# Where the sums of w2 run, in which order x and w1 are loaded, and when late statistics may start, in an FNet and MLP kernel

## The chip, the cores and the metric

The kernel runs on one core of one Trainium2 chip. The metric is the device time of one execution, in microseconds (us).

## The reference

The input x has 2048 rows (tokens) of 576 features. It is normalized, and the output is x plus two branches of the normalized xn:

```
xn = (x - mean) / sqrt(var + 1e-5)              # over the 576 features
a  = xn @ dft_hid_re.T ;  b = xn @ dft_hid_im.T  # Fourier branch
A  = dft_seq_re @ a - dft_seq_im @ b             # 2048 x 2048 matrices
B  = max(xn @ w1, 0) @ w2                        # w1 576 x 4608, w2 4608 x 576
out = x + A + B
```

All inputs are float32, and w1 and w2 have eight times the usual spread.

## The kernel before, in words

TensorE (PE) multiplies in float16. To keep the accuracy, an operand is scaled by a power of two and split into a high and a low float16 part: ScalarE writes the high part (L164), VectorE (DVE) the low part (L165), and PE forms three of the four products. The larger products also use Winograd's form of Strassen's scheme: of two 2 x 2 block matrices, 7 products instead of 8, with sums and differences of blocks as operands.

The MLP branch comes first. The 4608 hidden features are 9 blocks `b` of 512; the 2048 rows are 4 groups `g` of 512, each of 4 tiles `t` of 128 rows. A step (b, g) is `mlp1` (4 column tiles of w1, N=512, L286), `mlp1_out`, which turns a pair of its results into operands for Strassen, once for each of the two pairs (ReLU, high parts, low parts, sums, and last the difference L314 that gives the low part of the sums), and `mlp2`, 7 products (L328), each followed by an addition on VectorE into the accumulator `acc` (L334). The loop over steps issues `mlp1` of step n together with `mlp2` of step n-1.

What block 0 needs in addition is what the change is about:

- `load_x(t)` loads a tile of x into `acc`; `load_w1(b, i)` and `load_w2(b, i)` load halves of a block of w1 and w2 into one of two `raw` buffers, so that w2 waits until w1 has been split.
- `stats(ts)` takes mean and variance of tiles (L182 bn_stats, L185 aggregation), a square root on ScalarE (L192), and a chain of small VectorE steps (L193 to L204). `normalize` (L224 on VectorE, L225 on ScalarE), `remainder` (L229 and L232, on GpSimd, called POOL in the profile, except for tile 0) and `transposes` (9 on PE, L240, and two ScalarE copies out of PSUM, L245 and L248) then fill `xT[g]`. A group's `mlp1` needs the whole `xT[g]`; only for the first group and half of the second is it done tile by tile (`tile_by`).
- `max_w1` takes the largest magnitude of w1 (L98 on VectorE), `power_w1` makes the scale from it through PE (`power_pe`, L140 to L155), `split_w1` splits.
- `prepare_w2` sums magnitudes of w2 on ScalarE (L374), makes scales (`power_w2`), splits the first parts of w2 (`split_w2` with c=0), then forms the sums of w2's blocks in place (`sums_w2`, L404 to L407), and splits these (c=1 and 2). `mlp2` needs all of it.

Transposes, `mlp2` and `power_pe` share two PSUM buffers (`ps2`).

The text of the kernel is not the order on an engine. A scheduler at compile time orders each engine's instructions: the earlier in the text, the more urgent, but an instruction that its model takes to be ready goes ahead of one that isn't. `tc.issue_after(ins)` puts what a block issues on the engine of `ins` behind `ins` in that engine's order. On the chip each of VectorE, ScalarE and POOL works through its list in order.

Of the kernel before, what the change touches and what calls it, by code (L numbers as in the profile page):

```python
# [1 line left out]

# [7 lines left out]
F32 = mybir.dt.float32  # L10
BF16 = mybir.dt.bfloat16
I32 = mybir.dt.int32
AF = mybir.ActivationFunctionType
ALU = mybir.AluOpType
# [3 lines left out]
P = 128  # L18
# [10 lines left out]
TG = G // P  # L29
GH = G // 2  # L30
KT = 5
# [10 lines left out]
def kernel(  # L42
# [17 lines left out]
    nc = tc.nc  # L60

    const = ctx.enter_context(tc.tile_pool(name="const", bufs=1))
# [14 lines left out]
    raws = {}  # L77

    def load_x(t):
        nc.sync.dma_start(acc[t], x[t * P : (t + 1) * P, :])  # L80
# [2 lines left out]
        r = raws[key] = raw.tile(shape, F32, tag="raw", name="raw_" + "_".join(map(str, key)))  # L83
        nc.sync.dma_start(r, src)

    def load_w1(b, i, parts=1, eng=nc.sync):
        r = raws["w1", b, i] = raw.tile([P, 2 * KT, P], F32, tag="raw", name=f"raw_w1_{b}_{i}")
        n = 2 * KT // parts
        for k in range(0, 2 * KT, n):
            eng.dma_start(r[:, k : k + n], w1[b, i][:, k : k + n])  # L90

    def load_w2(b, i):
        load_raw(("w2", b, i), w2[b, i], [P, 4, EH])
# [2 lines left out]
    def magnitude(dst, src):  # L96

        nc.vector.tensor_reduce(dst, src, AX.XY, ALU.max, apply_absolute_value=True)  # L98
# [18 lines left out]
    idle = const.tile([P, 256], F16, name="idle")  # L117
# [41 lines left out]
    def cell(tag, n=NQ):  # L159
        return small.tile([P, n], F32, tag=f"c_{tag}", name=f"c_{tag}", bufs=2)  # L160
# [9 lines left out]
    means, factors, shifts, order = {}, {}, {}, {}  # L170

    eps = const.tile([P, 1], F32, name="eps")
    nc.vector.memset(eps, EPS)

    def stats(ts):

        n = len(ts)
        mv = small.tile([P, n, 2], F32, tag=f"mv{n}", name=f"mv{ts[0]}")
        sts = [small.tile([P, 2, 6], F32, tag="st", name=f"st{t}", bufs=4) for t in ts]
        for t, st in zip(ts, sts):  # L180
            for j in range(2):
                nc.vector.bn_stats(st[:, j, :], acc[t][:, j * EH : (j + 1) * EH])  # L182
                yield
        for i, st in enumerate(sts):
            nc.vector.bn_aggr(mv[:, i], st.rearrange("p a b -> p (a b)"))  # L185
            yield
        r0, u, r, sh = (
            small.tile([P, n], F32, tag=f"{a}{n}", name=f"{a}_{ts[0]}") for a in ("r0", "u", "r", "sh")
        )
        m, v = mv[:, :, 0], mv[:, :, 1]  # L190
        stt = nc.vector.scalar_tensor_tensor
        nc.scalar.activation(u, v, AF.Sqrt, bias=eps)  # L192
        nc.vector.reciprocal(r0, u)  # L193
        yield

        stt(u, v, EPS, r0, ALU.add, ALU.mult)
        yield
        nc.vector.tensor_tensor(u, u, r0, ALU.mult)
        yield
        nc.vector.tensor_scalar(u, u, -0.5 * SX, 1.5 * SX, ALU.mult, ALU.add)  # L200
        yield
        nc.vector.tensor_tensor(r, u, r0, ALU.mult)
        yield
        stt(sh, m, -1.0, r, ALU.mult, ALU.mult)  # L204
        for i, t in enumerate(ts):
            means[t], factors[t], shifts[t] = mv[:, i, 0:1], r[:, i : i + 1], sh[:, i : i + 1]

    def weave(steps, *others):

        others = list(others)  # L210
        for _ in steps:
            if others:
                others.pop(0)()
        for f in others:
            f()
# [80 lines left out]
    def mlp1_out(b, g, i, pa, pb):  # L296

        h = hs[b, g, i] = mlp.tile([P, 2, 7, GH], F16, tag="h", name=f"h{b}_{g}_{i}", bufs=4)
        st = mlp.tile([P, 5, GH], F32, tag="stage", name=f"s{b}_{g}_{i}")
        stt = nc.vector.scalar_tensor_tensor  # L300
        a11, a21, a12, a22 = pa[:, :GH], pa[:, GH:], pb[:, :GH], pb[:, GH:]
        r21, s1, s2, s3, s4 = (st[:, n] for n in range(5))
        nc.scalar.activation(r21, a21, AF.Relu)  # L303
        for q, src in ((slice(A11, A11 + 1), a11), (slice(A12, A22 + 1), pb)):
            hi, lo = (h[:, n, q].rearrange("p a b -> p (a b)") for n in range(2))
            nc.scalar.activation(hi, src, AF.Relu)  # L306
            stt(lo, src, 0.0, hi, ALU.max, ALU.subtract)  # L307
        stt(s3, a11, 0.0, r21, ALU.max, ALU.subtract)
        stt(s1, a22, 0.0, r21, ALU.max, ALU.add)
        stt(s2, a22, 0.0, s3, ALU.max, ALU.subtract)  # L310
        stt(s4, a12, 0.0, s2, ALU.max, ALU.subtract)  # L311
        hi, lo = (h[:, n, S1 : S4 + 1] for n in range(2))
        order["s"] = nc.scalar.activation(hi, st[:, 1:], AF.Copy).ins  # L313
        nc.vector.tensor_tensor(lo, st[:, 1:], hi, ALU.subtract)  # L314

    places = {}

# [21 lines left out]
    sc, pw, mx = {}, {}, {}  # L339

    def max_w1(b, f):

        i, r = divmod(f, 2)
        if f == 0:
            mx["w1", b], sc["w1", b], pw["w1", b] = cell("mw1"), cell("sw1"), cell("pw1")
        if r == 0:
            mx["f", b] = cell("mf", 2)
            mx["b", i] = small.tile([P, 1], BF16, tag=f"mb{i}", name=f"mb{b}_{i}") if b < 2 else None
        magnitude(mx["f", b][:, r : r + 1], raws["w1", b, i][:, r * KT : (r + 1) * KT])
        if r:  # L350
            m = mx["w1", b][:, i : i + 1] if b > 1 else mx["b", i]
            nc.vector.tensor_reduce(m, mx["f", b], AX.X, ALU.max)

    def power_w1(b, i):
        s, p = (t["w1", b][:, i : i + 1] for t in (sc, pw))
        if b > 1:
            power(s, p, mx["w1", b][:, i : i + 1])
        else:
            power_pe(s, p, mx["b", i])
# [40 lines left out]
    def sums_w2(b, i):  # L400

        b12, b11, b21, b22 = (raws["w2", b, i][:, n] for n in range(4))
        tt = (nc.vector if b > 1 else nc.gpsimd).tensor_tensor
        tt(b11, b12, b11, ALU.subtract)  # L404
        tt(b12, b22, b12, ALU.subtract)
        tt(b22, b22, b11, ALU.subtract)
        tt(b21, b21, b22, ALU.subtract)  # L407
# [35 lines left out]
        )  # L443


    load_w1(0, 0, 2, nc.scalar)
    warm = const.tile([P, 1], F32, name="warm")
    nc.scalar.activation(warm, eps, AF.Sqrt)
    load_x(0)
    load_x(1)  # L450
    load_w1(0, 1)
    for t in range(2, 2 * TG):
        load_x(t)
    load_w2(0, 0)
    load_w2(0, 1)
    for t in range(2 * TG, NT):
        load_x(t)

    V, GP = nc.vector, nc.gpsimd
    ps = [ps1.tile([P, G], F32, tag="ps1", name=f"p1_0_0_{i}") for i in range(NF)]  # L460
# [6 lines left out]
    no = lambda: None  # L467
    N, E, T = normalize, remainder, transposes

    for _ in range(32):  # L470
        nc.tensor.matmul(ps[3][:, :256], idle[:, :P], idle, start=True, stop=True)

    weave(stats([0]), no, no, no, lambda: max_w1(0, 0))
    N(0)
    max_w1(0, 1)
    E(0, V)
    power_w1(0, 0)
    T(0)
    split_w1(0, 0)
    tile_by(0, (0,), ps, WK0)  # L480
# [53 lines left out]
    def work():  # L534
        if todo:
            todo.pop(0)()
# [5 lines left out]
    def load_d(j):  # L542
        load_raw(("d", j), dft[:, :, j * EH : (j + 1) * EH], [P, KT, EH])
# [12 lines left out]
    def split_d(j):  # L556
        split(dsp[j][:, 0], dsp[j][:, 1], raws["d", j], sc["d"][:, j : j + 1])
# [47 lines left out]
    for n in range(1, len(steps)):  # L605
        b, g = steps[n]
        pb, pg = steps[n - 1]
        if g == 0 and b:
            if b + 1 < NB:
                todo += prepare_block(b + 1)  # L610
            else:
                todo += [lambda: (load_d(0), load_d(1)), lambda: None, new_d, lambda: None]
                for j in range(4):
                    todo += [lambda j=j: power_d(j), lambda j=j: split_d(j)]
                    if j < 2:
                        todo += [lambda j=j: load_d(j + 2), lambda: None]
                todo += [scales_d]
        if b == 0 and g + 1 < NG:
            weave(stats([(g + 1) * TG + i for i in range(TG)]))
        ps = []  # L620
        for i in range(NF):
            if n > 1 or i > 1:
                ps.append(mlp1(b, g, i))
                if i % 2:
                    mlp1_out(b, g, i // 2, *ps[-2:])
            if b == 0 and g + 1 < NG:
                t = (g + 1) * TG + i
                normalize(t)
                remainder(t, nc.gpsimd)
                transposes(t)  # L630
            if n == 2 and i == 2:
                todo += prepare_block(1)
            for _ in range(1 if b else 3):
                work()
            for q in range(2 * i, min(2 * i + 2, 7)):
                mlp2(pb, pg, q)
            for _ in range(1 if b else 3):
                work()
            if n > 3 and i % 2 and passes:
                passes.pop(0)()  # L640
# [115 lines left out]
    for n, (p, kh) in enumerate(units):  # L756
# [4 lines left out]
        for i, (q, rq, first, row, col) in enumerate(PRODUCTS):  # L761
# [5 lines left out]
            ps, w = places[PLACE[i]], csp[m]  # L767
            for k in range(HK):
                r = R[kh * HK + k]
                for j, (a, c) in enumerate(((0, 0), (0, 1), (1, 0))):  # L770
                    nc.tensor.matmul(  # L771
                        ps, w[:, a, k], r[:, c, rq],
                        start=first and k == 0 and j == 0, stop=k == HK - 1 and j == 2,
# [63 lines left out]
```

## Time and profile before

| | |
|---|---|
| median of 3 runs | 1306.94 us (1304.04 to 1307.52) |
| profiled execution: time | 1306.57 us |
| profiled execution: span | 1304.8 us |
| mean granted clock of PE | 0.991 |
| PE busy | 1274.5 us, 98% of the span |
| VectorE busy | 968.0 us, 74% |
| ScalarE busy | 532.8 us, 41% |
| POOL busy | 49.7 us, 4% |

The span is the time between the first and the last instruction of the profiled execution; the rest of its time, 1.77 us, lies around it. In rows of the trace, a row with times gives start and duration, engine, line, operation, what it writes and reads, and in brackets how long the engine had stood and what ended that. "Granted clock" is the share of full speed that PE was given.

### The profile page before, as it was taken

The numbers are of one execution on the slowest core, as the hardware profiler recorded it, in microseconds if no ns is written. First come the engines' busy times: TensorE is split into PE (matmuls) and PEld (weight loads), VectorE is DVE, ScalarE is ACT, GpSimd is POOL, SyncE is SP. The second block draws the span as 40 slices with busy tenths as digits, with TensorE's granted clock in tenths as the row PEclk, the third lists the DMA queues.
The fourth block names the chain that finished last, engine by engine and source line by source line (L and its number), as shares of the span: only waits on it lengthen the run. The fifth ranks groups of instructions, "written<-read, shape, count | busy, mean of one in ns | idle before, by whom it ended". The sixth has DMA issues, their size and how long they took to land.

```text
span 1304.8 us, 21675 instructions
## 1 busy us (share of the span) xinstructions
PE 1274.5 (98%) x9066; PEld 871.2 (67%) x9066; DVE 968.0 (74%) x1655; ACT 532.8 (41%) x794; POOL 49.7 (4%) x76
## 2 busy tenths in 40 slices
PE   7799999999999999999999999999999999999998
PEld 6565566666666666666666656677777777777777
DVE  8857778577596686785875885568678887878875
ACT  5634344344343443533433433234443333333332
POOL 2412000000000000000000000000000000000000
PEclk8899899999999999999999999999999999999999
DMA  6101213122122131131221222240014334243420
GB/s 238 42 1 55 76 49 116 58 73 87 48 89 85 49 107 68 49 125 49 74 93 41 94 94 85 91 149 17 1 52 172 131 128 159 98 146 121 142 84 19
DMA packets 38002, 112.75 MB, mean 86 GB/s; under 512 B 3984, under 2 KB 10640, under 8 KB 37904
## 3 DMA queue, kind: packets, MB, share of 16 engines
q1 hardware_dynamic: 37616, 110.71, 25.4%
q8 instruction: 71, 1.16, 0.4%
q10 hardware_dynamic: 288, 0.66, 0.1%
q14 instruction: 27, 0.22, 0.1%
HBM read 101.91 MB, written 9.44 MB: 85 GB/s over the span
## 4 chain that ended last, share of the span: by engine, by line
PE 89%; DVE 5%; ACT 2%; POOL 2%; DMA 1%; issue 1%; POOLq 0%; ACTq 0%; SPq 0%; DVEq 0%
PE p L286 30%; PE p L328 25%; PE p L771 25%; PE pd L670 8%; DVE acc L334 1%; DMA raw_d<-in_dft_dram 1%; ACT xT L245 0%; DVE h L314 0%; DVE w2s L165 0%; DVE h L307 0%; DMA raw_w<-in_w_dram 0%; POOL raw_w L407 0%; PE pt L240 0%; DVE c_md L98 0%; POOL raw_w L404 0%
## 5 line engine op out<-in xcount | busy, mean ns | idle before, releaser
L286 PE MATMUL p<-xT,w1s 128*128 128x512 f16 (+1 forms) x2268 | 466.3, 359 | 4.6 <-ACT xT L245 4.5
L328 PE MATMUL p<-w2s,h 128*128 128x288 f16 x3024 | 397.7, 288 | 14.3 <-ACT xT L248 7.8
L328 PEld LDWEIGHTS <-h 128*128 128x128 f16 x3024 | 296.8, 98 | 117.1 <-issue 15.3
L286 PEld LDWEIGHTS <-w1s 128*128 128x128 f16 x2268 | 210.0, 99 | 209.1 <-issue 9.1
L771 PE MATMUL p<-R,cs 128*128 128x288 f16 x2688 | 329.4, 287 | 0.0
L771 PEld LDWEIGHTS <-cs 128*128 128x128 f16 x2688 | 262.9, 98 | 66.3
L334 DVE SCALAR_TENSOR_TENSOR acc<-p,c_ub,acc 128x576 f32<-128x576 f32 x252 | 204.0, 812 | 19.3 <-PE p L328 18.9
L164 ACT ACTIVATE cs<-c,sc_c 128x1024 f16<-128x1024 f32 x112 | 128.5, 1148 | 202.0 <-PE p L771 147.6
L307 DVE SCALAR_TENSOR_TENSOR h<-p,h 128x256 f16<-128x256 f32 (+1 forms) x144 | 80.0, 555 | 148.6 <-ACT h L306 148.3
L165 DVE SCALAR_TENSOR_TENSOR cs<-c,sc_c,cs 128x1024 f16<-128x1024 f32 x112 | 143.7, 1283 | 50.2 <-ACT cs L164 42.9
L306 ACT ACTIVATE h<-p 128x256 f16<-128x256 f32 (+1 forms) x144 | 69.5, 485 | 236.9 <-PE p L286 236.9
L313 ACT ACTIVATE h<-s 128x1024 f16<-128x1024 f32 x72 | 76.1, 1058 | 166.6 <-DVE s L311 166.3
L670 PE MATMUL pd<-dsp,xT 128*128 128x288 f16 x896 | 109.9, 287 | 0.9 <-DVE acc L334 0.9
L314 DVE TENSOR_TENSOR h<-s,h 128x1024 f16<-128x1024 f32 x72 | 88.9, 1235 | 28.7 <-ACT h L313 28.6
L670 PEld LDWEIGHTS <-xT 128*128 128x128 f16 x896 | 87.6, 98 | 23.2 <-issue 1.1
L777 DVE SCALAR_TENSOR_TENSOR o<-p,us_c,o 128x288 f32<-128x288 f32 x112 | 57.5, 513 | 20.3 <-PE p L771 20.3
L598 ACT ACTIVATE f<-f 128x1024 f32<-128x1024 f32 x64 | 66.6, 1041 | 3.6 <-DMA f<-in_cre_dram 3.6
L165 DVE SCALAR_TENSOR_TENSOR w2s<-raw_w,c_sw,w2s 128x576 f16<-128x576 f32 (+1 forms) x54 | 48.2, 940 | 16.0 <-ACT w2s L164 16.0
L164 ACT ACTIVATE w2s<-raw_w,c_sw 128x576 f16<-128x576 f32 (+1 forms) x54 | 44.4, 850 | 36.7 <-DVE c_sw L396 19.0
L303 ACT ACTIVATE s<-p 128x256 f32<-128x256 f32 x72 | 26.7, 370 | 24.0 <-PE p L286 24.0
L688 ACT ACTIVATE R<-pd,c_rho 128x288 f16<-128x288 f32 x48 | 23.8, 499 | 22.2 <-DVE T L682 12.4
L165 DVE SCALAR_TENSOR_TENSOR w1s<-raw_w,c_sw,w1s 128x640 f16<-128x640 f32 x36 | 30.9, 878 | 0.1
(100 smaller groups left out, 623.8 us busy)
## 6 DMA issues: line engine op xcount, KB each, us to landing
f<-in_cre_dram SPq DMA_DIRECT2D x32, 512.0 KB, 3.5
f<-in_cim_dram SPq DMA_DIRECT2D x32, 512.0 KB, 3.5
c<-in_cre_dram SPq DMA_DIRECT2D x32, 512.0 KB, 3.9
c<-in_cim_dram SPq DMA_DIRECT2D x32, 512.0 KB, 4.5
raw_w<-in_w_dram SPq DMA_DIRECT2D x17, 640.0 KB, 4.0
raw_w<-in_w_dram SPq DMA_DIRECT2D x18, 576.0 KB, 4.0
acc<-in_x_dram SPq DMA_DIRECT2D x16, 288.0 KB, 6.1
spill<-acc SPq DMA_DIRECT2D x16, 288.0 KB, 2.5
```

Source lines behind the costliest of these rows:

```text
L164: nc.scalar.activation(hi, src, AF.Copy, scale=s)
L165: nc.vector.scalar_tensor_tensor(lo, src, s, hi, ALU.mult, ALU.subtract)
L286: nc.tensor.matmul(ps[:, cols], w1s[b, i // 2][:, hl, i % 2 * KT + k], xT[g][:, kx, cols], start=(n == 0), stop=(n == len(WK) - 1),)
L306: nc.scalar.activation(hi, src, AF.Relu)
L307: stt(lo, src, 0.0, hi, ALU.max, ALU.subtract)
L313: order["s"] = nc.scalar.activation(hi, st[:, 1:], AF.Copy).ins
L314: nc.vector.tensor_tensor(lo, st[:, 1:], hi, ALU.subtract)
L328: nc.tensor.matmul(ps[:, c], h[:, x, qa, c * P : (c + 1) * P], w[:, y, qb], start=first and i == 0 and j == 0, stop=i == NQ - 1 and j == 2 ...
L334: nc.vector.scalar_tensor_tensor(o, ps, us[b], o, ALU.mult, ALU.add)
L598: nc.scalar.activation(f, f, AF.Abs, scale=2.0**-10, accum_out=sums_c[:, n, q : q + 1])
L670: nc.tensor.matmul(ps[j], xT[g][:, kx, c * P : (c + 1) * P], dsp[j][:, hl, k], start=(n == 0), stop=(n == len(XK) - 1),)
L771: nc.tensor.matmul(ps, w[:, a, k], r[:, c, rq], start=first and k == 0 and j == 0, stop=k == HK - 1 and j == 2, skip_group_check=not first,)
```

## The change

Four things are done:

- `sums_w2` runs on VectorE for all blocks; before, blocks 0 and 1 ran it on POOL.
- The first half of w1 is loaded from SP's queue, like x, and no longer from ScalarE's: tile 0 of x, w1 in two parts, tiles 1 and 2 of x, the second half of w1, the other tiles.
- The statistics of the third and fourth group are put behind `order["lo"]`, the last difference (L314) of the pair that was issued last in the text, in VectorE's order. For the third group this is the first pair of step (0, 1), for the fourth the second pair of it. The maxima of w1 of block 1 are put behind it too: its first half behind the first pair of step (0, 2), its second half behind the second pair.
- 14 more matmuls on an idle tile stand between the first scale of w1 and the transposes of tile 0.

```diff
-    def load_w1(b, i, parts=1, eng=nc.sync):
+    def load_w1(b, i, parts=1):
...
-            eng.dma_start(r[:, k : k + n], w1[b, i][:, k : k + n])
+            nc.sync.dma_start(r[:, k : k + n], w1[b, i][:, k : k + n])
...
-        nc.vector.tensor_tensor(lo, st[:, 1:], hi, ALU.subtract)
+        order["lo"] = nc.vector.tensor_tensor(lo, st[:, 1:], hi, ALU.subtract).ins
...
-        magnitude(mx["f", b][:, r : r + 1], raws["w1", b, i][:, r * KT : (r + 1) * KT])
+        with tc.issue_after(order["lo"]) if b == 1 else nullcontext():
+            magnitude(mx["f", b][:, r : r + 1], raws["w1", b, i][:, r * KT : (r + 1) * KT])
...
-        tt = (nc.vector if b > 1 else nc.gpsimd).tensor_tensor
+        tt = nc.vector.tensor_tensor
...
-    load_w1(0, 0, 2, nc.scalar)
-    warm = const.tile([P, 1], F32, name="warm")
-    nc.scalar.activation(warm, eps, AF.Sqrt)
     load_x(0)
+    load_w1(0, 0, 2)
     load_x(1)
+    load_x(2)
     load_w1(0, 1)
-    for t in range(2, 2 * TG):
+    for t in range(3, 2 * TG):
         load_x(t)
...
+    warm = const.tile([P, 1], F32, name="warm")
+    nc.scalar.activation(warm, eps, AF.Sqrt)
...
-    for _ in range(32):
-        nc.tensor.matmul(ps[3][:, :256], idle[:, :P], idle, start=True, stop=True)
+    def fill(n):
+
+        for _ in range(n):
+            nc.tensor.matmul(ps[3][:, :256], idle[:, :P], idle, start=True, stop=True)
+
+    fill(32)
...
     power_w1(0, 0)
+    fill(14)
     T(0)
...
         if b == 0 and g + 1 < NG:
-            weave(stats([(g + 1) * TG + i for i in range(TG)]))
+            with tc.issue_after(order["lo"]):
+                weave(stats([(g + 1) * TG + i for i in range(TG)]))
```

More of the change, by code (lines that the diff above doesn't have):

```diff
@@ L1 @@
-from contextlib import ExitStack
+from contextlib import ExitStack, nullcontext
 import concourse.bass as bass
```

## The prediction

> **What bounds the kernel now.** I read the page's busy times first, then a table of stretches, then the waits of PE, then the order of time at the two places where PE waited longest.
>
> ```profile
> span 1304.8 us, 21675 instructions
> PE 1274.5 (98%) x9066; PEld 871.2 (67%) x9066; DVE 968.0 (74%) x1655; ACT 532.8 (41%) x794; POOL 49.7 (4%) x76
> ```
>
> PE is the bound of the whole: 1304.8 - 1274.5 leaves 30.3 us in which it did nothing. The other engines matter only where they make PE idle, or cold. The stretches say where that is (columns: busy time and count of PE, PEld, DVE, ACT, POOL; granted clock; DMA share; GB/s):
>
> ```profile
> 0.00:20.00 20.00, 13.67 (x110) 10.76 (x110) 16.44 (x70) 9.36 (x15) 1.61 (x6) 0.83 0.86 311
> 20.00:40.00 20.00, 17.43 (x293) 16.38 (x292) 19.00 (x67) 16.68 (x30) 9.29 (x12) 1.00 0.23 79
> 40.00:60.00 20.00, 12.36 (x100) 7.74 (x98) 14.53 (x27) 13.34 (x22) 14.30 (x16) 0.85 0.17 52
> 60.00:80.00 20.00, 17.05 (x128) 11.52 (x127) 15.09 (x32) 9.02 (x15) 4.79 (x8) 0.89 0.04 15
> 80.00:100.00 20.00, 20.00 (x145) 12.61 (x143) 10.20 (x20) 6.63 (x12) 0.86 (x1) 1.00 0.00 1
> 120.00:140.00 20.00, 16.06 (x79) 8.51 (x78) 15.36 (x27) 5.38 (x9) 9.05 (x9) 0.83 0.20 66
> 200.00:400.00 200.00, 200.00 (x1254) 122.52 (x1253) 147.90 (x280) 80.75 (x139) 2.84 (x8) 1.00 0.25 82
> ```
>
> From 200 us on PE is full and at clock 1.00. Nearly all that can be won lies in the first 140 us: 19.49 us idle in the first 80, 3.94 in 120 to 140, and more where the clock is 0.83 to 0.89. The change touches nothing that PE waits for later (from the third block on the sums of w2 are on VectorE already). From 20 to 40 us DVE is 95% busy and is the likely limit; from 40 to 60 and from 120 to 140 PE and DVE are both idle in part while POOL works, the mark of a chain through POOL.
>
> The waits of PE in the first 140 us (total, times, longest), and the order of time at the two longest:
>
> ```profile
> PE p L328 <- ACT xT L248: 7.8, 2, 6.9
> PE p L328 <- DVE acc L334: 3.9, 2, 3.4
> ```
>
> ```profile
> 46.92 1.60 POOL L404 TENSOR_TENSOR raw_w<-raw_w 128x288 f32<-128x288 f32 x1 [2.19 <-DVE w2s L165]
> ...
> 54.67 1.19 POOL L407 TENSOR_TENSOR raw_w<-raw_w 128x288 f32<-128x288 f32 x1
> 55.89 0.78 ACT L164 ACTIVATE w2s<-raw_w,c_sw 128x576 f16<-128x576 f32 x1 [1.75 <-POOL raw_w L407]
> 56.58 0.26 ACT L248 ACTIVATE xT<-pt 128x128 f16<-128x128 f16 x1
> 56.88 5.00 PE L328 MATMUL p<-w2s,h 128*128 128x288 f16 x24 [6.86 <-ACT xT L248]
> ...
> 128.29 1.37 POOL L407 TENSOR_TENSOR raw_w<-raw_w 128x288 f32<-128x288 f32 x1
> 129.70 0.77 ACT L164 ACTIVATE w2s<-raw_w,c_sw 128x576 f16<-128x576 f32 x1 [1.94 <-POOL raw_w L407]
> 130.50 0.82 DVE L165 SCALAR_TENSOR_TENSOR w2s<-raw_w,c_sw,w2s 128x576 f16<-128x576 f32 x1 [1.49 <-ACT w2s L164]
> 132.50 0.81 DVE L334 SCALAR_TENSOR_TENSOR acc<-p,c_ub,acc 128x576 f32<-128x576 f32 x1
> 133.37 3.04 PE L328 MATMUL p<-w2s,h 128*128 128x288 f16 x12 [3.40 <-DVE acc L334]
> ```
>
> Block 0: the sums on POOL run from 46.92 to 55.86. ScalarE's splits wait for them one by one, and behind the last in ScalarE's order stands L248, a 0.26 us copy that frees the PSUM buffer PE waits for. PE stood 6.86 us. Block 1: the same through DVE. Its w2 split waits for ScalarE, that for POOL, and the addition at 132.50 which frees PE's next buffer is queued behind: 3.40 us. After such a stop PE is slow:
>
> ```profile
> 57.00:60.50 3.50, 3.50 (x16) 2.18 (x15) 1.91 (x2) 2.26 (x5) 1.42 (x2) 0.50 0.60 196
> 133.40:139.20 5.80, 5.80 (x20) 2.73 (x20) 5.80 (x12) 1.60 (x3) 0.38 (x1) 0.50 0.15 64
> ```
>
> At half clock, 3.5 us cost 1.75 us and 5.8 us cost 2.9 us on top of the stops.
>
> **The change, part by part.** The sum is made against the profiled execution's own 1306.57 us, which lies 0.37 us below the median of the runs shown (1306.94). The rows of its terms follow; the stretches show PE alone (length, busy, count, clock, DMA share, GB/s):
>
> ```profile
> 13.20:43.70 30.50, 26.16 (x408) 0.95 0.34 116
> 43.70:74.26 30.56, 20.75 (x148) 0.89 0.14 44
> 118.00:140.00 22.00, 18.06 (x94) 0.84 0.18 60
> ```
>
> ```profile
> L404 DVE TENSOR_TENSOR raw_w<-raw_w x14: 447/450/460, 190.8 to 728.2; 128x288 f32<-128x288 f32 x14
> L182 DVE BATCH_NORM_STATS2 st<-acc 128x6 f32<-128x288 f32 x19 | 7.4, 442 | 0.0
> L224 DVE TENSOR_SCALAR xn<-acc,mv,r 128x576 f32<-128x576 f32 x6 | 3.2, 576 | 0.0
> L185 DVE BATCH_NORM_AGGREGATE mv<-st 128x2 f32<-128x12 f32 x12 | 1.4, 172 | 0.0
> L98 DVE TENSOR_REDUCE c_mf<-raw_w 128x1 f32<-128x640 f32 x4 | 3.2, 805 | 0.0
> L232 POOL TENSOR_TENSOR xn<-xn 128x512 f16<-128x512 f32 x15 | 18.0, 1198 | 0.0
> L229 POOL TENSOR_TENSOR xn<-xn 128x64 f16<-128x64 f32 x15 | 5.1, 340 | 47.1 <-ACT xn L225 43.3 <-DVE xn L224 3.9
> ```
>
> ```profile
> 59.11 1.60 DVE L314 TENSOR_TENSOR h<-s,h 128x1024 f16<-128x1024 f32 x1 [1.59 <-ACT h L313]
> 61.36 0.41 DVE L307 SCALAR_TENSOR_TENSOR h<-p,h 128x256 f16<-128x256 f32 x1
> 62.76 0.69 DVE L307 SCALAR_TENSOR_TENSOR h<-p,h 128x512 f16<-128x512 f32 x1
> ```
>
> The group rows (count, busy us, mean ns of one) are the sums' line over the whole run, bn_stats, normalization and aggregation from 20 to 36 us, the maxima from 44 to 74.3, and POOL's remainders from 0 to 140. A pair's h on DVE, `mlp1_out`, is the last three rows' 1.60 + 0.41 + 0.69 and four sums of 256 columns like the one of 0.41: 4.3 us.
>
> *Loads and start.*
>
> ```profile
> 4.58 0.82 DVE L182 BATCH_NORM_STATS2 st<-acc 128x6 f32<-128x288 f32 x2 [1.32 <-DMA acc<-in_x_dram]
> 6.57 0.82 DVE L98 TENSOR_REDUCE c_mf<-raw_w 128x1 f32<-128x640 f32 x1 [0.34 <-DMA raw_w<-in_w_dram]
> 1.04 6.16 PE L471 MATMUL p<-idle 128*128 128x256 f16 x32 [1.04 <-DVE idle L118]
> 13.23 3.14 PE L286 MATMUL p<-xT,w1s 128*128 128x128 f16 x28 [1.11 <-ACT xT L245]
> ```
>
> Today x and w1 come on two queues and arrive mixed: tile 0 of x is used at 4.58, the second half of w1 at 6.57. On one queue x's 288 KB should be through alone, then 640 KB of w1, and tile 1 of x no longer lies between the halves of w1. If bytes move as fast as now, the later of these arrivals, 6.57, needs 928 KB moved in place of 1216: a quarter less of the some 4.5 us of moving, 0 to 1.2 us; I take 0.8. The issues of w1 move from ScalarE's queue to SP's, behind one x issue; tile 2 of x now goes ahead of the second w1 tile, which the first products don't use. [...]
>
> The 14 idle matmuls between the first power and the first transposes: 6.16 / 32 = 0.19 us each, 2.7 us, in a place where PE waits anyway; they may hold up the first transposes by some tenths. In return the first 28 products, 3.14 us, may run at full clock; if they run at half now, like the matmuls after the two stops, that is up to 1.6 us. But the next step on PE waits for the remainder of tile 1 on POOL, so I take 0.2 (bounds +0.5 and -1.6). [...]
>
> *Late statistics gated.* The 19 bn_stats between 20 and 36 us are 3 of the second group and 16 of the third and fourth, which DVE took in early: 16 x 0.442 = 7.1 us, with 8 aggregations x 0.172 = 1.4 us, in a stretch in which DVE never stands. They sit between the steps of the second group's reciprocal chain. Now the third group's wait for the last difference of step (0,1)'s first pair, the fourth's for that of its second pair. PE's loss from 13.2 to 43.7 is 30.50 - 26.16 = 4.3 us idle and about 1.5 us of clock (0.05 x 30.5): at most 5.8 us can come back. The transposes also go through POOL (1.198 + 0.340 us a tile) and ScalarE, which the gate does not relieve, so I take 2 (bounds 0 and 5). Up to 43.7, with the start: **-3.0**.
>
> *The sums on VectorE, block 0, up to the start of the third group's products (74.26).* Eight sums cost 8 x 0.45 = 3.6 us on DVE instead of 8.9 on POOL (46.92 to 55.86). The POOL chain and the 6.86 us stop go. What is late next is DVE. It gets the 3.6 us of sums, the third group's statistics, 8 x 0.442 + 4 x 0.172 and six small steps of about 0.17, together 5.2 us, and its 4 normalizations, 2.3 us. It loses the 4 maxima of block 1, 3.2 us, and the fourth group's small chain and two normalizations, 2.1 us, which stand there now. It was busy 14.53 + 15.09 of 40 us, so about 23 of these 30.6, and needs 23 + 3.6 + 5.2 + 2.3 - 5.3 = 28.8 us; less what can follow the third group's transposes (a pair's h and an addition, 5 us), plus the way of the last tile through POOL and PE, about 3 us, it is 26.8. DVE will not pack without gaps, so I take 27.5 us in place of 30.56, **-3.0** (bounds: 19, PE's 20.75 less 1.75 of cold time, and 40.9, the slower rival).
>
> *Block 1's sums.* PE loses 22.0 - 18.06 = 3.94 us and 2.9 us of clock: 6.8 us. With 0.45 us sums the chain of eight is 3.6 us, no split waits for POOL, and the addition isn't held. DVE has 15.36 of 20 busy there and takes 3.6 more, so some of it may remain as DVE delay: **-5.0** (bounds 0 and -6.8).
>
> *Moved behind 74.* The fourth group's statistics and block 1's maxima, 5.2 + 3.2 = 8.4 us of DVE, now fall where DVE is busy 10.20 of 20 (80 to 100). The 9.8 us idle there hide them: **0**; without that cover PE would wait for the statistics at least, up to +5 us. A gate is an order on DVE alone: what is queued behind it is the chain to ScalarE's root, POOL's remainders and PE's transposes of that group.
>
> Sum: -3.0 - 3.0 - 5.0 + 0 = -11.0; 1306.57 - 11.0 = 1295.6 us.
>
> **Rivals.** *Slower: the gate makes the third group late.* If the difference it waits for ends no sooner than today (59.11 + 1.60 = 60.7), then 5.2 us of statistics, 0.58 of the first normalization, 4 x 1.54 us of POOL and 2 us to the transposed tile come to 74.6, no gain; with the second pair's h and seven additions of 0.81 ahead of them on DVE (4.3 + 5.7 = 10.0 us), 84.6, which is 10.3 us late, and PE cold again for 1.75 us more. Less block 1's 5.0 and the start's 0.8 that is +6.2: 1312.8. It decides for slower once the third group's products start after about 80 us (74.26 + 5.8). For it: DVE is the engine that gets work. Against: with the 7.1 + 1.4 us of filler no longer ahead of it, and no POOL between, that difference should fall near 52. Chance 0.10.
>
> *No change: the stop moves.* ScalarE's order keeps L248 late, or PE's order puts a transpose behind the gate, so that block 0 gains nothing, and uncovered late statistics take 4 of block 1's 5 us: 1306.57 - 0.8 - 1.0 = 1304.8. Chance 0.14.
>
> *The gate does nothing.* If the differences come so early that nothing is held back, the early fillers stay, and with them the 2 us; 1297.6. Chance 0.06.
>
> *More than forecast.* If DVE packs as well as the bounds allow: -5 up to 43.7, -6 after it, -6.8 in block 1: 1288.8. Chance 0.12.
>
> **How the numbers follow.** The forecast has 0.58, so faster by over 0.3% (3.9 us, about what a measurement of this kernel can tell from no change) has 0.58 + 0.06 + 0.12 = 0.76, within it 0.14, slower 0.10. The range from 1288 to 1307 leaves out the slower rival, half of the larger gain's tail and a little of the middle case.
>
> **What would show it.** Right: no sums of w2 on POOL; the wait of PE for L248 under 2 us and for the addition in block 1 under 1; clock 1.00 from 130 to 140; third group's products at 66 to 70 instead of 74.26; PE's idle time near 22 us. Wrong: a new long wait of PE for xT between 50 and 85 us behind bn_stats (the slower rival), or DVE full and PE idle between 75 and 118 (the cover is gone).

## The result, and the profile after

The changed kernel takes 1309.59 us (median of 13 runs, 1307.77 to 1310.26), the kernel before 1306.68 us in the same comparison (13 runs). The ratio is 1.0027, with a 95% interval from 1.0018 to 1.0035: some 3 us slower (2.9 by the medians, 3.5 by the ratio), where 11 us faster was forecast. The profiled execution took 1310.21 us, with a span of 1308.4. Page and stretches of the profile after (columns as before):

```profile
span 1308.4 us, 21689 instructions
PE 1273.3 (97%) x9080; PEld 872.4 (67%) x9080; DVE 973.5 (74%) x1671; ACT 532.5 (41%) x794; POOL 34.6 (3%) x60
```

```profile
0.00:20.00 20.00, 12.97 (x102) 9.54 (x103) 17.06 (x71) 8.07 (x14) 1.62 (x6) 0.93 0.85 293
20.00:40.00 20.00, 19.43 (x308) 19.10 (x307) 11.89 (x31) 16.82 (x30) 9.40 (x12) 0.90 0.27 97
40.00:60.00 20.00, 9.71 (x86) 5.79 (x83) 18.87 (x46) 9.94 (x16) 0.00 (x0) 0.87 0.22 67
60.00:80.00 20.00, 13.05 (x90) 9.40 (x91) 15.08 (x46) 8.57 (x13) 9.77 (x12) 0.70 0.00 0
80.00:100.00 20.00, 18.60 (x139) 11.91 (x137) 10.10 (x16) 8.38 (x14) 3.05 (x4) 1.00 0.01 2
118.00:140.00 22.00, 20.91 (x131) 12.28 (x130) 19.50 (x42) 10.20 (x18) 0.00 (x0) 1.00 0.19 57
```

Three things changed. From 20 to 40 us VectorE fell from 19.00 to 11.89 us busy: the late statistics left. PE rose from 17.43 to 19.43 us busy, but at clock 0.90 in place of 1.00, so that it got through only 308 matmuls in place of 293. From 118 to 140 us PE lost 1.09 us in place of 3.94, at clock 1.00 in place of 0.84. But from 40 to 80 us PE was busy 22.76 us in place of 29.41, and in the second half of this the clock was 0.70 in place of 0.89. The waits of PE in the first 140 us name it; their first row is

```profile
PE pt L240 <- ACT xn L225: 16.0, 2, 13.4
```

a wait for a normalized tile; the kernel before has only one such wait there, of 1.9 us. The stop for L248 went, as forecast (6.9 us before, 0.8 now). In order of time around it, and below that the third group's first products in the kernel before:

```profile
43.10 7.83 PE L286 MATMUL p<-xT,w1s 128*128 128x128 f16 x56 [1.00 <-ACT xT L245]
54.62 0.81 DVE L165 SCALAR_TENSOR_TENSOR w2s<-raw_w,c_sw,w2s 128x576 f16<-128x576 f32 x1
56.28 1.21 DVE L314 TENSOR_TENSOR h<-s,h 128x1024 f16<-128x1024 f32 x1
57.41 2.97 DVE L182 BATCH_NORM_STATS2 st<-acc 128x6 f32<-128x288 f32 x8
62.81 1.55 DVE L224 TENSOR_SCALAR xn<-acc,mv,r 128x576 f32<-128x576 f32 x3
63.42 2.37 ACT L225 ACTIVATE xn<-acc,sh,r 128x576 f16<-128x576 f32 x3
64.33 0.61 PE L240 MATMUL pt<-ident,xn 128*128 128x128 f16 x4 [13.40 <-ACT xn L225]
67.05 0.61 PE L240 MATMUL pt<-ident,xn 128*128 128x128 f16 x4 [1.05 <-POOL xn L232]
67.46 6.28 PE L328 MATMUL p<-w2s,h 128*128 128x288 f16 x32
84.80 3.18 PE L286 MATMUL p<-xT,w1s 128*128 128x512 f16 x14 [0.61 <-ACT xT L245]
```

```profile
74.26 4.87 PE L286 MATMUL p<-xT,w1s 128*128 128x512 f16 x14 [1.11 <-ACT xT L245]
```

PE finishes the first-layer products of step (0, 1) at 50.9 and stands until 64.33. What it stands for is the first transpose of the third group. The gated statistics of that group start at 57.41, right behind the difference L314 that they were put behind. Yet the 84 products of `mlp2` of step (0, 0) (L328) need nothing of them: the last split of w2 that they use ended at 55.43, and some could have run before that. They are behind the transpose in PE's order, which was fixed at compile time. They run from 67.46 on, the first 32 of them in 6.28 us at a granted clock of 0.65, and the third group's products start at 84.80 in place of 74.26.

### The profile page after: what moved, and what is told of

Its sections match the earlier page's. It is cut to its first block, busy times and chain, and to the rows that moved or that the text cites. A ratio compares the mean times of both kernels' runs of the same rounds, so it can differ in the third digit from the quotient of the medians.

```text
span 1308.4 us, 21689 instructions
## 1 busy us (share of the span) xinstructions
PE 1273.3 (97%) x9080; PEld 872.4 (67%) x9080; DVE 973.5 (74%) x1671; ACT 532.5 (41%) x794; POOL 34.6 (3%) x60
## 4 chain that ended last, share of the span: by engine, by line
PE 88%; DVE 6%; DMA 2%; ACT 2%; issue 1%; POOL 0%; SPq 0%; POOLq 0%; DVEq 0%; ACTq 0%
PE p L286 29%; PE p L328 26%; PE p L779 24%; PE pd L678 8%; DVE acc L334 1%; DVE w2s L165 1%; DMA raw_d<-in_dft_dram 1%; ACT xT L245 1%; DMA c<-in_cim_dram 1%; DVE h L307 0%; DMA acc<-in_x_dram 0%; PE pt L240 0%; DVE st L182 0%; DVE cs L165 0%; DVE c_md L98 0%
## 5 line engine op out<-in xcount | busy, mean ns | idle before, releaser
L328 PE MATMUL p<-w2s,h 128*128 128x288 f16 x3024 | 396.9, 287 | 3.5 <-DVE acc L334 2.3
L328 PEld LDWEIGHTS <-h 128*128 128x128 f16 x3024 | 296.2, 98 | 105.3 <-issue 4.3
L306 ACT ACTIVATE h<-p 128x512 f16<-128x512 f32 (+1 forms) x144 | 69.7, 486 | 226.4 <-PE p L286 224.1
L314 DVE TENSOR_TENSOR h<-s,h 128x1024 f16<-128x1024 f32 x72 | 87.9, 1221 | 29.0 <-ACT h L313 29.0
L240 PE MATMUL pt<-ident,xn 128*128 128x128 f16 x144 | 12.1, 227 | 20.2 <-ACT xn L225 16.0
```

The lines of the kernel that those rows point to most:

```text
L314: order["lo"] = nc.vector.tensor_tensor(lo, st[:, 1:], hi, ALU.subtract).ins
L328: nc.tensor.matmul(ps[:, c], h[:, x, qa, c * P : (c + 1) * P], w[:, y, qb], start=first and i == 0 and j == 0, stop=i == NQ - 1 and j == 2 ...
```

## The experiments

Theory A, formed from this trace: the gate on the third group's statistics makes the loss, because a transpose that waits for it stands ahead of ready products in PE's order; the sums on VectorE gain. Theory B: VectorE is full there, and nothing on PE matters. Theory C: the sums on VectorE lose. All times are medians; ratios are to the kernel before, measured beside each, with 95% intervals.

**The statistics free** (from the changed kernel):

```diff
-            with tc.issue_after(order["lo"]):
-                weave(stats([(g + 1) * TG + i for i in range(TG)]))
+            weave(stats([(g + 1) * TG + i for i in range(TG)]))
```

> The kernel after the change, with the third and fourth groups' statistics free again (no gate); all else as changed. Theory A (the gate costs: the third group's first transpose stands ahead of ready products in PE's order and waits for gated statistics): 1298 to 1300 us, no wait of PE over 3 us between 50 and 65, third group's products at 72 to 75 us instead of 84.8. Theory B (VectorE is simply full there, gate or not): 1303 to 1306. Theory C (the sums on VectorE cost, not the gate): 1308 or more.

Measured: 1299.07 us, 0.9948 (0.9934 to 0.9961). In order of time on PE:

```profile
48.98 1.63 PE L328 MATMUL p<-w2s,h 128*128 128x288 f16 x12 [1.56 <-ACT xT L248]
57.09 4.51 PE L328 MATMUL p<-w2s,h 128*128 128x288 f16 x24 [2.60 <-DVE s L311]
72.90 3.18 PE L286 MATMUL p<-xT,w1s 128*128 128x512 f16 x14 [0.82 <-ACT xT L245]
```

The long wait is gone, and the third group's products start 11.9 us earlier than in the changed kernel. Against it the gate costs 1.0027 / 0.9948, 0.8%, some 10 us. Theory C falls.

**The gate kept, another order on PE.** The third group's transposes are issued behind the last product of `mlp2(0, 0)`:

```diff
-                transposes(t)
+                if n != 1:
+                    transposes(t)
...
             for q in range(2 * i, min(2 * i + 2, 7)):
                 mlp2(pb, pg, q)
+            if n == 1 and i == NF - 1:
+                with tc.issue_after(order["pe"]):
+                    for k in range(TG):
+                        transposes(2 * TG + k)
...
-                    nc.tensor.matmul(
+                    order["pe"] = nc.tensor.matmul(
...
-                    )
+                    ).ins
```

> The kernel after the change with the gate kept, but the third group's transposes put behind the last product of step (0,0) in PE's order. Theory A: the 13.4 us wait goes although the statistics are as late as before; third group's products at 73 to 76 us, 1299 to 1301 us. Theory B: the products of step (0,0) run earlier, but the third group's start stays over 82 us, since VectorE's order decides it: 1307 to 1309. Theory C: within 2 us of the changed kernel.

Measured: 1301.88 us, 0.9975 (0.9966 to 0.9984).

```profile
54.81 4.78 PE L328 MATMUL p<-w2s,h 128*128 128x288 f16 x24 [2.16 <-DVE s L311]
61.29 4.57 PE L328 MATMUL p<-w2s,h 128*128 128x288 f16 x36 [1.69 <-DVE acc L334]
68.09 0.67 PE L240 MATMUL pt<-ident,xn 128*128 128x128 f16 x9
74.24 5.72 PE L286 MATMUL p<-xT,w1s 128*128 128x512 f16 x15 [1.11 <-ACT xT L245]
```

The products now fill the time in which the transpose waited, and the third group starts at 74.24, near where it started before the change, though its statistics are gated as in the changed kernel (they start at 57.26 here and at 57.41 there). From 50.93 to 64.33, where PE stood in the changed kernel, it is busy 9.55 us. So two thirds of the gate's cost, 1.0027 - 0.9975 of 1.0027 - 0.9948, was PE's order. That is Theory A, and B falls.

**The same order without the gate**, both edits together, for the rest:

> No gate on the statistics, and the third group's transposes behind the last product of step (0,0) in PE's order. With the gate this order gave 1301.88 us, without the gate the usual order gave 1299.07. If late statistics alone (VectorE) cost the difference of 2.8 us between these: 1297.5 to 1299.5. If it is the price of the forced order on PE: 1301 to 1303.

Measured: 1300.26 us, 0.9963 (0.9951 to 0.9976). It lies between the two alternatives. The interval overlaps with that of the free statistics in the usual order and with that of the gate in the new order, so how the last 2 to 3 us divide between late statistics and the forced order stays open. The profiles show where they lie: with the gate and the new order the third group's first 15 products took 5.72 us (14 took 3.18 with the statistics free and the usual order), and without the gate but with the new order they started at 76.15, 3.25 us later than in the usual order.

**One gate at a time** (`if g == 1 else nullcontext()` on the gate for the third group alone, `g == 2` for the fourth alone):

> The kernel after the change with only the third group's statistics gated, the fourth's free. Theory A: the third group's gate is the whole loss: 1308 to 1310.5 us, a wait of PE for a transpose of over 10 us, third group's products at 83 to 86 us. If the fourth group's gate carries part of the loss: 1303 to 1307.

> The kernel after the change with only the fourth group's statistics gated, the third's free. Theory A: no loss (the cover of 80 to 100 us): 1297.5 to 1300.5 us. If late statistics cost wherever they fall: 1302 to 1306.

Measured: third alone 1310.59 us, 1.0042 (1.0029 to 1.0056); fourth alone 1299.84 us, 0.9962 (0.9949 to 0.9974). The wait of PE for a normalized tile (first the one, then the other):

```profile
PE pt L240 <- ACT xn L225: 16.4, 2, 13.8
```

```profile
PE pt L240 <- ACT xn L225: 2.6, 1, 2.6
```

The third group's gate is the whole loss. The fourth's is covered, as forecast; a cost of 0.14% can't be told from none here.

**The gate alone**, on the kernel before, sums still on POOL (`order["lo"]` set, the gate as in the diff of the change):

> The kernel before with the gate on the third and fourth groups' statistics alone, sums on POOL. Theory A: the gate costs about as much as in the changed kernel or more, since the difference it waits for ends later: 1313 to 1317 us, a wait of PE for a transpose of 12 to 16 us near 50 to 66. If the gate hurts only together with the sums on VectorE: 1304 to 1308.

Measured: 1316.22 us, 1.0079 (1.0066 to 1.0093). Its wait, and the second part of tile 4's transposes:

```profile
PE pt L240 <- ACT xn L225: 17.5, 2, 15.6
29.07 0.40 PE L240 MATMUL pt<-ident,xn 128*128 128x128 f16 x4 [0.18 <-POOL xn L232]
```

The gate costs 0.8% with either engine for the sums. It does what it was expected to do early: tile 4's transposes end at 29.5 where they ended at 30.6 before, since VectorE no longer takes in late statistics. But that 1 us is not kept here: tile 7's products start at 42.10, and at 41.97 in the kernel before. The 15.6 us wait is what the gate takes.

**The sums**, once put back on POOL in the changed kernel, once moved alone in the kernel before:

```diff
-        tt = nc.vector.tensor_tensor
+        tt = (nc.vector if b > 1 else nc.gpsimd).tensor_tensor
```

> The kernel after the change with the sums of w2 of blocks 0 and 1 back on POOL. Theories A and B (the sums on VectorE gain, the gate loses): slower than the changed kernel by 5 to 8 us, 1314 to 1317, with PE's stop near 130 us back (3 to 4 us, then half clock). Theory C: 1302 to 1305, faster than the changed kernel.

> The kernel before with one edit, all sums of w2 on VectorE. Theories A and B: 1297 to 1301 us: block 1's stop of 3.4 us and its 2.9 us of half clock go, and block 0's stop of 6.9 us shrinks to under 3. Theory C: 1307 to 1310, with VectorE as what PE waits for at 50 to 60 us.

Measured: back on POOL 1317.13 us, 1.0094 (1.0080 to 1.0108); moved alone 1297.25 us, 0.9941 (0.9927 to 0.9954). With the sums back on POOL, PE's stop in block 1 is back, later in time, since that whole kernel is late:

```profile
144.69 3.04 PE L328 MATMUL p<-w2s,h 128*128 128x288 f16 x12 [3.40 <-DVE acc L334]
```

From the kernel with the sums moved alone, the stretch of block 1, and PE at two places:

```profile
118.00:140.00 22.00, 21.53 (x137) 13.18 (x135) 21.93 (x43) 8.83 (x14) 0.96 (x2) 1.00 0.19 61
```

```profile
56.38 4.77 PE L328 MATMUL p<-w2s,h 128*128 128x288 f16 x24 [3.99 <-DVE s L311]
71.99 3.18 PE L286 MATMUL p<-xT,w1s 128*128 128x512 f16 x14 [1.11 <-ACT xT L245]
```

PE loses 0.47 us in block 1's stretch in place of 3.94, at a granted clock of 1.00; VectorE is busy 21.93 of 22 us there, and still it carries the eight sums. In block 0 the stop of 6.86 us becomes one of 3.99, where under 3 was expected, now for the other of the two shared PSUM buffers (freed by L311, the last sum of the pair), and the third group starts 2.27 us earlier. So the sums are worth 0.6% to 0.7%, 8 to 9 us, alone or together with the rest.

**The small parts**, each added to the kernel with the sums moved alone (1297.25 us): the load order, the 14 idle matmuls, the gate on block 1's maxima, and the first two together.

> The kernel before with all sums of w2 on VectorE (1297.25 us alone) and the load order of the change. The prediction's term (tile 0 of x and w1 earlier, -0.8): 1296 to 1297. The rival (tile 1 of x, now behind w1, arrives later and gives the time back at the second tile): 1297 to 1299, first products 0.5 to 1 us earlier than 13.1, the second tile's products no earlier than 18.4.

> The kernel before with all sums of w2 on VectorE and the 14 idle matmuls. If the clock at the start is on the path: first products in 1.7 us instead of 3.14 and 1295.5 to 1296.5. The rival (the second tile waits for POOL anyway, PE stands there instead, and the clock is lost a little later): 1297 to 1298.5, with the 56 products near 18.4 us slower than 3.54.

> The kernel before with all sums of w2 on VectorE and the gate on block 1's maxima alone. Theory A and the prediction's term (the cover of 80 to 100 us hides them): 1296.5 to 1298. The rival (block 1's chain from maxima to w2 gets late and PE waits in its step): 1299 to 1302.

> The kernel before with the sums on VectorE, the load order and the 14 idle matmuls, no gate at all: what of the change doesn't lose. If the two small parts add up: 1295 to 1297 us. If they take from each other, as the changed kernel's start does (first products at 11.9 us, second tile's at 19.5 and slow): 1297 to 1299.

| added to the sums | us | ratio (interval) |
|---|---|---|
| load order | 1296.31 | 0.9930 (0.9917 to 0.9943) |
| idle matmuls | 1296.74 | 0.9933 (0.9920 to 0.9946) |
| gate on the maxima | 1297.36 | 0.9933 (0.9921 to 0.9945) |
| load order and idle matmuls | 1297.55 | 0.9939 (0.9926 to 0.9951) |

None can be told from 0.9941: the medians lie within 1 us of 1297.25, and the intervals leave room for 2 to 3 us more or less. So none of these alternatives is decided by the time alone. With the load order the first products start earlier (12.34 in place of 13.12) and the second tile's later (19.91 in place of 18.38), as the rival there had it. The trace of the load order shows the second half of w1, and that of the idle matmuls the first and second products:

```profile
7.05 0.82 DVE L98 TENSOR_REDUCE c_mf<-raw_w 128x1 f32<-128x640 f32 x1 [1.44 <-DMA raw_w<-in_w_dram]
```

```profile
12.90 1.72 PE L286 MATMUL p<-xT,w1s 128*128 128x128 f16 x28 [1.11 <-ACT xT L245]
18.26 4.91 PE L286 MATMUL p<-xT,w1s 128*128 128x128 f16 x56 [1.01 <-ACT xT L245]
```

What of the change is worth keeping is thus the sums on VectorE. That kernel, with or without the small parts, beats both the kernel before and the changed one.

## Why the prediction was wrong, step by step

Without the third group's gate the change gains 0.4% to 0.5%, 5 to 7 us (1299.84 us with the fourth's gate, 1299.07 with neither), about half of the 11 us that were forecast. With the gate it loses.

- **Block 1's sums, -5.0: right.** PE's loss in the stretch fell from 3.94 to 1.09 us and the half clock went (granted 1.00 over the stretch in place of 0.84): 5.75 us of the 6.8.
- **Moved behind 74, 0: right.** The fourth group's gate alone and the gate on the maxima alone cost nothing that can be told.
- **Up to 43.7, -3.0: wrong, about +1.** The trace has tile 7's products start at 43.10 in place of 41.97. The filler between the second group's steps cost about 1 us, not 2: from the end of the second tile's products to tile 7's it takes 18.1 us in the changed kernel and 19.2 with the statistics free. On the kernel before, the gate alone kept nothing of it by tile 7. The start lost more than that:

```profile
3.68 0.82 DVE L182 BATCH_NORM_STATS2 st<-acc 128x6 f32<-128x288 f32 x2 [0.42 <-DMA acc<-in_x_dram]
6.43 0.82 DVE L98 TENSOR_REDUCE c_mf<-raw_w 128x1 f32<-128x640 f32 x1 [0.74 <-DMA raw_w<-in_w_dram]
11.92 1.72 PE L286 MATMUL p<-xT,w1s 128*128 128x128 f16 x28 [1.30 <-ACT xT L245]
11.93 0.29 ACT L192 ACTIVATE u<-mv,eps 128x1 f32<-128x1 f32 x1
16.27 0.63 PE L240 MATMUL pt<-ident,xn 128*128 128x128 f16 x5 [2.62 <-ACT xn L225]
19.51 5.48 PE L286 MATMUL p<-xT,w1s 128*128 128x128 f16 x56 [1.00 <-ACT xT L245]
```

Tile 0 of x came 0.9 us earlier, the second half of w1 only 0.14 us. The first products started 1.3 us earlier and took 1.72 us at a granted clock of 1.00, in place of 3.14 at 0.50. But tile 1's square root went to ScalarE at 11.93, behind the copies of tile 0; PE stood 2.62 us, and the next 56 products took 5.48 us at a granted clock of 0.58. In this execution VectorE stood 0.13 us ahead of tile 1's first statistics, at 7.63; the rest of the work on that tile stands later in the orders of VectorE and ScalarE. The prediction looked at tile 0's path and at w1, not at tile 1, which the new order puts behind w1.

- **Block 0 up to the third group's start, -3.0: wrong, +9.4** (41.70 us from tile 7's products to the third group's, in place of 32.29; with the 1.1 us from before that, the third group is 10.5 us late). This is the step that failed. It counted VectorE's work and let PE follow. That VectorE would be full there was right: it was busy 12.86 of the 13.0 us from 51 to 64 in the changed kernel. What the step left out is PE's own order. "What can follow the third group's transposes" was counted for VectorE, but on PE the products of step (0, 0) did follow them, without need. PE stood 13.40 us, of which it works 9.55 with the transposes behind these products, and some 2 us of slow clock came after (32 products in 6.28 us at a granted 0.65, where 44 a little later took 5.55 at 1.00). The difference that the gate waits for ended at 57.5, not at 52: all eight sums and the last splits of w2 were placed ahead of it. The -3.0 was too large even without this fault: the same stretch gains 1.2 us with the gate and the new order on PE (31.09), 2.4 with the statistics free (29.87) and 2.3 with the sums moved alone (30.03).

The slower rival named the place and the size (third group's products at 84.6; measured 84.80; 1312.8 us against 1310.21), but by another mechanism: additions ahead of the statistics on VectorE, where in fact no addition ran, since PE, whose products they add, stood. The true one, "PE's order puts a transpose behind the gate", stood as half a sentence in the rival of no change, priced there as no gain in block 0, not as a loss. That is where the chance was misplaced: the text saw which engine would be full, and not which engine would be stopped by its own order.

From 85 us on the changed kernel wins back 7 us: 5.75 in block 1, and 1.7 of clock that the kernel before lost from 74.2 to 79.2 (granted 0.66) after its stops, less 1.0 for a new wait near the end, and 0.5 because tile 12's transposes are among those done before the third group's start. That is how +10.5 at the third group ends as +3.6 between the two profiled executions.

## What to carry to other kernels

Here an edge in VectorE's order was paid by PE, which stood 13.40 us with ready products behind a transpose in its own order: before adding such an edge, list on each engine what stands behind the first instruction that needs the gated result, and move ready work ahead of it in the same change. The work that filled in ahead of need on busy VectorE cost about 1 us here, the stop of PE, the bounding engine, 13.40. A change of several parts can hold a gain and a larger loss; here one part is worth -8 us, another +10, and each shows alone.

## What the runs showed of the hardware

PE's slow clock at the start was moved, not removed. The kernel before ran its first 28 products in 3.14 us (granted clock 0.50) and the 56 of the second tile, at 1.00, in

```profile
18.38 3.54 PE L286 MATMUL p<-xT,w1s 128*128 128x128 f16 x56 [0.96 <-ACT xT L245]
```

With the idle matmuls it is 1.72 us and 4.91, in the changed kernel 1.72 (granted 1.00) and 5.48 (0.58). Between the two PE then stood 2.36 us (0.61, 0.74 and 1.01) and 4.36 us (2.62, 0.74 and 1.00), in the kernel before 0.96. With the load order alone both are slow, 3.14 and 4.90, with 2.79 us of standing between them (1.19, 0.60 and 1.00). In five traces with the 14 idle matmuls (the changed kernel, the statistics free, the gate with the new order on PE, the sums back on POOL, and the idle matmuls alone) the first products took 1.72 us and the second 4.91 to 5.64. The kernel with free statistics and the new order on PE has the 14 matmuls too and begins as the changed kernel does, and still its first products were slower:

```profile
11.94 2.70 PE L286 MATMUL p<-xT,w1s 128*128 128x128 f16 x28 [1.30 <-ACT xT L245]
```

What makes the first products take 2.70 us in one execution and 1.72 in another is not shown. The slow second products, five times of five, do not look like chance. One execution of each kernel cannot show how often the one or the other falls.

One queue did not bring w1 reliably earlier. Its second half was used at 6.57 us in the kernel before, at 6.45 with the sums moved alone and at 6.46 with the idle matmuls alone, all three with two queues and 288 KB more ahead of it by the prediction's count. With one queue it was used at 6.43 in the changed kernel and at 7.05 with the load order alone. In the changed kernel it landed at 6.4 us, 4.8 after its issue, in the kernel before at 6.5, 5.4 after it. The bytes did not move as fast as in the kernel before, which the prediction's 0.8 us supposed: in the first 8 us the DMA moved 226 GB/s in the changed kernel and 283 before. The first loads on SP's queue landed in the order of issue in the changed kernel: tile 0 of x at 3.6 us, the two parts of w1 at 4.5 and 6.4, tile 1 of x at 7.6 (2.9, 3.4, 4.8 and 5.5 us after their issues). Tile 0 of x was used at 3.68 in place of 4.58, but the gain for w1 that the prediction took did not come.

A difference of 1024 columns on VectorE (L314) took 1.60 us beside POOL's remainders in the kernel before (at 59.11) and 1.21 us with POOL at rest (the changed kernel, at 56.28). In the first case a step of POOL was under way when it started. In the changed kernel's L314 at 64.28 it was the other way round: the difference took 1.22 us, and the step of POOL that started just after it 1.31, where the next of its kind (at 66.96) took 0.30:

```profile
64.35 1.31 POOL L229 TENSOR_TENSOR xn<-xn 128x64 f16<-128x64 f32 x1 [30.93 <-ACT xn L225]
```
